# Another order of attention steps, loads and first MLP units in a fused decay-attention and MLP kernel

## The chip, the cores and the metric

The kernel runs on one NeuronCore of a Trainium2 chip. The metric is the time of one execution in device microseconds, as the median of several runs. The engines have the names of the profile: PE (TensorE), DVE (VectorE), ACT (ScalarE), POOL (GpSimd) and SP (SyncE, which issues nearly all DMAs here).

## The reference

Attention with a decaying state, in blocks of 64 positions, for 2 batches of 8 heads with 768 positions of 64 features; then two MLPs over the 1536 tokens of 512 features.

```python
for b in range(nb):
    intra = np.einsum('bhic,bhjc->bhij', qb, kb) * Dmask[None]      # lam ** (i - j), causal
    intra = np.einsum('bhij,bhjd->bhid', intra, vb)
    inter = np.einsum('bhid,bhde->bhie', qb * lam_pow[None], kv_state)
    out[:, :, sl] = intra + inter
    kv_state = lam_block[None, :, None, None] * kv_state + np.einsum('bhsd,bhse->bhde', kb * rev_pow[None], vb)
...
g = x @ w_gate; x = (g * sigmoid(g) * (x @ w_val)) @ w_out          # d_ff 1536
h = x @ w_in;   out = (h * np.cos(h)) @ w_out                       # d_ff 2048
```

Everything is float32. The kernel writes each MLP operand as the sum of a high and a low part in a shorter format and makes each product from three matmuls.

## The kernel before

**Attention.** It works in 12 chunks (numbers 0 to 11, six of each batch) of 128 positions with all heads. A chunk needs three loads of 256 KiB, q, k and v, and six steps on PE, which the code names by a letter and the chunk: `t` transposes q and k in halves of 64 rows (line 1079), `s` makes the scores (1097), `d` the addition to the state (1104), `a` scores times v (1110), `c` q times state (1119; chunks 0 and 6 have none, chunks 5 and 11 no `d`). `m` makes the decay mask once (1088). Between them ACT copies the transposed tiles out of PSUM (tile `qkt`), DVE multiplies the scores with the mask (tile `at`) and updates the state, and POOL makes the decayed copies `kd`, `qd` and `stmp`. The result of a chunk is the MLP input x, split in high and low parts by ACT and DVE.

**MLPs.** The tokens are three blocks of 512 (0, 1, 2). The first units are plain: `gate` and `val`, each for two columns of weights (f = 0, 1) and three blocks, 12 units of 12 matmuls of 512 columns. After them blocks 0 and 1 go together through products of the seven-product kind (Strassen and Winograd's): `q` in the first MLP and `r` in the second, with seven pieces named b, a, c, d, 2, 3, 4, six matmuls of 512 columns each; block 2 does the same with 256 columns, as `h` and `w`. The piece `r.d.12` is piece d of kind r for the weights 12; it adds to the PSUM bank of `r.c.12`, which ACT must have copied out first. Between the pieces stand the down projections, groups of three matmuls. DVE and ACT turn every unit's result into the operand of a down projection, and every loaded weight into its two parts.

**Who sets the order.** The program is written by a scheduler in the kernel that runs at build time: it keeps a clock for each engine, prices each operation and always emits the one that can start first. Each engine then runs its list in order. Three tables steer it. `STEPS` gives the order of attention steps, with `u` where an MLP unit may stand. `LOADS` ranks the loads of q, k, v and the first weights (G0, V0, G1, V1: gate and val for f = 0, 1). `units` lists the units in order. Where the scheduler expects PE to idle for over 1 us before an attention step, it puts in matmuls on zeros (line 234), one for each 115 ns of it. Prices of loads include pauses of 1 us at the times in `FETCHES`.

```python
turn_of = {(names[o[0]], int(o[1:])): n - 1000 for n, o in enumerate(LOADS.split())}
...
BUFS = {"q": 3, "k": 3, "v": 5, "qkt": 2, "qd": 3, "kd": 2, "at": 2, "stmp": 2}
```

Of the kernel before, what the change touches and what calls it, by code (L numbers as in the profile page):

```python
# [47 lines left out]
EARLY = 4  # L48
LATENCY = 130
ISSUE = 400  # L50
STALL, FETCHES = 1000, (13000, 20600, 29000, 36500, 45000, 54500, 63500)
BEHIND = 7000
ATT_NS = {"t": 470, "mask": 700, "s": 892, "st": 464, "av": 875, "qs": 440}
TILES = {"mask": "32", "t": "64*128", "s": "64*128", "st": "128*64", "av": "128*64", "qs": "64*64"}
STEPS = (
# [3 lines left out]
)  # L59
LOADS = (  # L60
    "q0 k0 k1 q1 q3 k2 q4 q2 k3 q5 v0 k4 k6 k5 v1 v2 q6 k7 v3 v4 G0 v5 k8 q7 v6 q8 "
    "v8 v7 k9 q9 q10 k10 k11 q11 V0 v9 v11 v10 V1 G1"
)
HELD = 6, 7, 8, 9
BUFS = {"q": 3, "k": 3, "v": 5, "qkt": 2, "qd": 3, "kd": 2, "at": 2, "stmp": 2}
# [7 lines left out]
def kernel(  # L73
# [222 lines left out]
    ]  # L296
    first2 = len(downs)
    units = [(nm, blk, f) for f in range(GROUP1) for nm in ("gate", "val") for blk in range(NBLK - 1)]
    units += [(nm, NBLK - 1, f) for f in range(GROUP1) for nm in ("gate", "val")]
    parts = "bcad234"  # L300

# [45 lines left out]
    def matrix(kind, f):  # L347

        if kind in "qh":
            return tuple((nm, f) for nm in ("gate", "val", "sa", "sb"))  # L350
        return ("in2", f), ("in2", f + 1), ("ta", f), ("tb", f)

    def work(op):

        if op[0] in ATT_NS:
            return ATT_NS[op[0]] / 1360
        if op[0] in ("h", "w"):
# [55 lines left out]
    for key in list(first_use):  # L413
        if key[0] in ("sa", "sb", "ta", "tb"):
            m = matrix("q" if key[0] in FIRST else "r", key[1])
# [191 lines left out]
    def switch(sub):  # L607

        kind = sub["op"][0]
        if TILES.get(kind) != last_tiles[0]:  # L610
            return SWITCH.get(kind, 145)
        return 60 if last_tiles[1] and kind not in ATT_NS else 0

    def small(sub):

        return sub["op"][0] in ("h", "w")
# [26 lines left out]
    def run_pe(sub, end, idle):  # L643

        unit = any(sub is s for s in pe_units)
        last_small[0] = small(sub)
        last_tiles[:] = TILES.get(sub["op"][0]), sub["op"][0] in ATT_NS
        for subs in (pe_att, pe_units, pe_downs):
            subs[:] = [s for s in subs if s is not sub]
        items = []  # L650
        for _ in range(int(sub["bank"])):
# [3 lines left out]
            if unit:  # L655
                unit_banks.add(item[1])
        sub["fn"](*(items or [None]), **({"idle": idle} if idle and sub["op"][0] in ATT_NS and items else {}))
        for key in sub["keys"]:
# [395 lines left out]
    def att_sub(op):  # L1054
# [92 lines left out]

        return dict(ns=ATT_NS[kind], needs=needs, keys=[], bank=n, fn=fn, then=then, clock=seen[op], op=op)

# [513 lines left out]
```

## Time and profile before

| | |
|---|---|
| time, median of 3 runs (lowest to highest) | 591.8 us (591.25 to 592.13) |
| the profiled execution | 590.59 us |
| its span, first to last instruction | 588.8 us |
| PE busy | 578.5 us, 98% |
| DVE, ACT, POOL busy | 506.0, 362.5, 34.1 us |
| granted TensorE clock, mean | 0.999 |

Busy time is that in which an engine has an instruction at work. The profiled execution is 1.2 us under the median, and 1.8 us of it lie outside the span. The profile's lines are L numbers of the kernel before; the changed kernel's are one higher from line 299 on.

### The profile page before, as it was taken

The numbers are of one execution on the slowest core, as the hardware profiler recorded it, in microseconds if no ns is written. First come the engines' busy times: TensorE is split into PE (matmuls) and PEld (weight loads), VectorE is DVE, ScalarE is ACT, GpSimd is POOL, SyncE is SP. The second block draws the span as 40 slices with busy tenths as digits, with TensorE's granted clock in tenths as the row PEclk, the third lists the DMA queues.
The fourth block names the chain that finished last, engine by engine and source line by source line (L and its number), as shares of the span: only waits on it lengthen the run. The fifth ranks groups of instructions, "written<-read, shape, count | busy, mean of one in ns | idle before, by whom it ended". The sixth has DMA issues, their size and how long they took to land.

```text
span 588.8 us, 9643 instructions
## 1 busy us (share of the span) xinstructions
PE 578.5 (98%) x3620; PEld 491.8 (84%) x3620; DVE 506.0 (86%) x943; ACT 362.5 (62%) x689; POOL 34.1 (6%) x50
## 2 busy tenths in 40 slices
PE   8999999999999999999999999999999999989997
PEld 5888888888888888888888888888888888868886
DVE  4688899878889889786979999969799999999973
ACT  3554767757567557454453679876568667857641
POOL 5646000000000000000000000000000000000000
PEclk9999999999999999999999999999999999999999
DMA  9999362554585554543441522301212031300013
GB/s 189 211 210 212 113 147 71 162 144 147 175 225 185 156 146 140 170 128 141 129 142 51 180 89 72 107 2 39 70 37 71 1 108 37 108 0 1 1 74 141
DMA packets 72816, 66.68 MB, mean 113 GB/s; under 512 B 40002, under 2 KB 60738, under 8 KB 72770
## 3 DMA queue, kind: packets, MB, share of 16 engines
q1 hardware_dynamic: 72768, 66.07, 40.2%
q8 instruction: 28, 0.46, 0.3%
q14 instruction: 18, 0.15, 0.1%
q10 hardware_dynamic: 2, 0.00, 0.0%
HBM read 54.00 MB, written 12.06 MB: 112 GB/s over the span
## 4 chain that ended last, share of the span: by engine, by line
PE 84%; DVE 11%; ACT 2%; DMA 1%; issue 1%; SPq 0%; ACTq 0%; DVEq 0%
PE bank L154 21%; PE bank L155 21%; PE bank L156 20%; PE bank L1493 5%; PE bank L1494 5%; PE bank L1495 5%; DVE s L529 2%; DVE sum L529 2%; PE bank L1110 2%; PE bank L1097 2%; DVE wl L541 1%; DMA v<-in_v_dram 1%; PE bank L1119 1%; PE bank L1079 1%; PE bank L1104 1%; DVE s L1241 1%
## 5 line engine op out<-in xcount | busy, mean ns | idle before, releaser
L154 PE MATMUL bank<-xl,wh 128*128 128x512 f32 (+1 forms) x336 | 118.4, 352 | 3.0 <-ACT s L536 3.0
L536 ACT ACTIVATE s<-s 128x512 f32<-128x512 f32 (+2 forms) x124 | 73.4, 594 | 75.2 <-DVE s L529 47.5
L155 PE MATMUL bank<-xh,wh 128*128 128x512 f32 (+1 forms) x336 | 117.7, 350 | 0.0
L156 PE MATMUL bank<-xh,wl 128*128 128x512 f32 (+1 forms) x336 | 117.3, 349 | 0.0
L536 ACT ACTIVATE s<-bank 128x512 f32<-128x512 f32 (+2 forms) x126 | 62.5, 500 | 36.4 <-PE bank L156 30.8
L536 ACT ACTIVATE gh<-s 128x512 fp32r<-128x512 f32 x84 | 52.7, 628 | 38.7 <-DVE s L529 35.3
L529 DVE TENSOR_TENSOR s<-bank,s 128x256 f32<-128x256 f32 (+1 forms) x102 | 57.3, 563 | 22.2 <-PE bank L156 21.3
L154 PE MATMUL bank<-wl,gh 128*128 128x512 f32 (+1 forms) x196 | 75.6, 386 | 0.0
L155 PE MATMUL bank<-wh,gh 128*128 128x512 f32 (+1 forms) x196 | 75.6, 386 | 0.0
L156 PE MATMUL bank<-wh,gl 128*128 128x512 f32 (+1 forms) x196 | 75.5, 385 | 0.0
L154 PEld LDWEIGHTS bank<-xl,wh 128*128 128x128 f32 x336 | 63.6, 189 | 12.7 <-ACT s L536 3.7
L156 PEld LDWEIGHTS bank<-xh,wl 128*128 128x128 f32 x336 | 63.6, 189 | 8.4
L155 PEld LDWEIGHTS bank<-xh,wh 128*128 128x128 f32 x336 | 63.7, 190 | 8.1
L529 DVE TENSOR_TENSOR sum<-bank,sum 128x512 f32<-128x512 f32 (+1 forms) x97 | 63.2, 681 | 8.1 <-PE bank L156 5.8
L536 ACT ACTIVATE wh<-ct 128x512 fp32r<-128x512 f32 x91 | 55.5, 627 | 23.8 <-DVE ct L205 20.2
L541 DVE TENSOR_TENSOR wl<-ct,wh 128x512 fp32r<-128x512 f32 x91 | 61.3, 688 | 6.9 <-ACT wh L536 6.2
L529 DVE TENSOR_TENSOR gl<-s,gh 128x512 fp32r<-128x512 f32 x84 | 57.7, 689 | 6.3 <-ACT gh L536 5.9
L1493 PE MATMUL bank<-gh,wl 128*128 128x512 f32 x144 | 56.2, 390 | 0.0
L1494 PE MATMUL bank<-gh,wh 128*128 128x512 f32 x144 | 56.2, 390 | 0.0
L1495 PE MATMUL bank<-gl,wh 128*128 128x512 f32 x144 | 56.1, 389 | 0.0
L193 ACT ACTIVATE ct<-raw 128x512 f32<-128x512 f32 x68 | 44.9, 668 | 7.6 <-DMA raw<-in_moe_w_out_dram 4.4
L205 DVE SCALAR_TENSOR_TENSOR ct<-ct,raw 128x512 int32<-128x512 int32 x68 | 46.4, 689 | 3.1 <-ACT ct L193 1.3
(169 smaller groups left out, 1034.7 us busy)
## 6 DMA issues: line engine op xcount, KB each, us to landing
raw<-in_moe_w_out_dram SPq DMA_DIRECT2D x28, 512.0 KB, 3.6
raw<-in_moe_w_in_dram SPq DMA_DIRECT2D x16, 512.0 KB, 3.8
raw<-in_moe_w_gate_dram SPq DMA_DIRECT2D x24, 256.0 KB, 4.6
raw<-in_moe_w_val_dram SPq DMA_DIRECT2D x24, 256.0 KB, 4.5
draftout<-raw SPq DMA_DIRECT2D x9, 512.0 KB, 2.6
q<-in_q_dram SPq DMA_DIRECT2D x12, 256.0 KB, 5.2
k<-in_k_dram SPq DMA_DIRECT2D x12, 256.0 KB, 5.3
v<-in_v_dram SPq DMA_DIRECT2D x12, 256.0 KB, 5.7
```

The lines of the kernel that those rows point to most:

```text
L154: nc.tensor.matmul(ps, wh, xl, start=first, stop=False, **kw)
L155: nc.tensor.matmul(ps, wh, xh, start=False, stop=False, **kw)
L156: nc.tensor.matmul(ps, wl, xh, start=False, stop=last, **kw)
L193: nc.scalar.activation(t, words[:, :, 1].bitcast(F32), AF.Prelu, scale=2.0 ** -112, alpha=2.0 ** 32)
L205: nc.vector.scalar_tensor_tensor(out=w, in0=w, scalar=3, in1=lo, op0=ALU.logical_shift_left, op1=ALU.bitwise_or)
L529: engine, 66 + n * 1.047 if engine == "DVE" else n * 2.45, lambda: unit.tensor_tensor(out=out, in0=in0, in1=in1, op=op),
L536: return go("ACT", (175 if fn == AF.Silu else 40) + n * 0.94, lambda: nc.scalar.activation(out, src, fn, **kw))
L541: return "any", {"DVE": 66 + n * 1.047, "POOL": n * 2.45}, lambda e: (nc.vector if e == "DVE" else nc.gpsimd).tensor_tensor(out=out, in0=i ...
L1097: nc.tensor.matmul(ps[:, p * C:(p + 1) * C], kt[r, p, :], qt[r, p, :], start=True, stop=True)
L1493: nc.tensor.matmul(ps, lo[:, cs], gh, start=first, stop=False)
L1494: nc.tensor.matmul(ps, hi[:, cs], gh, start=False, stop=False)
L1495: nc.tensor.matmul(ps, hi[:, cs], gl, start=False, stop=last)
```

## The change

Three tables and one list change. `FETCHES` and `ATT_NS` are prices in the scheduler's clock and set no wait by themselves. `units[:4]` puts the gate and val units of f = 0 first, for block 0 and then block 1, where before both gate units of f = 0 came first. Six units stand among the attention steps where three stood.

```diff
-STALL, FETCHES = 1000, (13000, 20600, 29000, 36500, 45000, 54500, 63500)
+STALL, FETCHES = 1000, (13471, 21050, 27114, 34715, 41507, 53380, 64222, 69133)
-ATT_NS = {"t": 470, "mask": 700, "s": 892, "st": 464, "av": 875, "qs": 440}
+ATT_NS = {"t": 490, "mask": 700, "s": 892, "st": 464, "av": 875, "qs": 440}
 STEPS = (
-    "t0 m s0 t1 a0 t2 s1 d0 s2 d1 a1 t3 t4 a2 s3 d2 c2 c1 d3 a3 d4 c3 t5 s4 t6 s5 "
...
+    "t0 m s0 t1 s1 t2 d0 s2 t3 a0 a1 d1 s3 c1 t4 d2 a2 c2 d3 a3 t5 s4 c3 s5 d4 a4 "
...
 LOADS = (
...
+units[:4] = [(nm, blk, 0) for blk in range(2) for nm in ("gate", "val")]
```

The instructions of both programs are the same on every engine but for two things: four more matmuls on zeros (44 for 40, with their weight loads), and one `wl` subtraction of 512 columns that goes from DVE to POOL (line 541). All else is order.

**SP, the first loads.** Tile numbers are given by chunk in order of their buffers: q_182, k_183, v_184 are chunk 0, q_185, k_186, v_187 chunk 1, q_188, k_189, v_190 chunk 2. Before:

```order
L936 DMA q_182<-in_q_dram 128x8x64
L936 DMA k_183<-in_k_dram 128x8x64
L936 DMA k_186<-in_k_dram 128x8x64
L936 DMA q_185<-in_q_dram 128x8x64
L936 DMA k_189<-in_k_dram 128x8x64
L936 DMA q_188<-in_q_dram 128x8x64
L936 DMA q_222<-in_q_dram 128x8x64
L936 DMA v_184<-in_v_dram 128x8x64
L936 DMA v_187<-in_v_dram 128x8x64
```

Of the changed kernel, the same place:

```order
L937 DMA q_182<-in_q_dram 128x8x64
L937 DMA k_183<-in_k_dram 128x8x64
L937 DMA q_188<-in_q_dram 128x8x64
L937 DMA k_189<-in_k_dram 128x8x64
L937 DMA k_186<-in_k_dram 128x8x64
L937 DMA q_185<-in_q_dram 128x8x64
L937 DMA q_222<-in_q_dram 128x8x64
L937 DMA v_187<-in_v_dram 128x8x64
L937 DMA v_184<-in_v_dram 128x8x64
L937 DMA v_190<-in_v_dram 128x8x64
L937 DMA k_267<-in_k_dram 128x8x64
```

Chunk 1's q goes from the 4th to the 6th place and chunk 0's v from the 8th to the 9th; chunk 3's k (k_267) is 11th. The last load of attention moves from the 40th place to the 44th, behind G1 and V1.

**PE, the first steps.** Of each step the first matmul of each kind stands. Before:

```order
L1097 MATMUL bank6_247<-qkt_221 128x128
...
L1079 MATMUL bank0_262<-anti_90,q_185 128x64
...
L234 MATMUL bank2_298<-zeros_92 128x256
...
L1110 MATMUL bank2_298<-at_257,v_184 64x128 x4
...
L1079 MATMUL bank4_335<-anti_90,q_188 128x64
...
L1097 MATMUL bank0_359<-qkt_280 128x128
...
L1104 MATMUL bank1_374<-v_184,kd_283 64x64 x8
```

Of the changed kernel; the zero matmuls are 9, 12 and 9 here, and 26 above:

```order
L1098 MATMUL bank6_247<-qkt_221 128x128
...
L234 MATMUL bank0_269<-zeros_92 128x256
...
L1080 MATMUL bank0_269<-anti_90,q_185 128x64
...
L234 MATMUL bank2_305<-zeros_92 128x256
...
L1098 MATMUL bank2_305<-qkt_296 128x128
...
L1080 MATMUL bank4_330<-anti_90,q_188 128x64
...
L1105 MATMUL bank6_353<-v_184,kd_263 64x64 x8
...
L234 MATMUL bank1_385<-zeros_92 128x256
...
L1080 MATMUL bank1_385<-anti_90,q_222 128x64
...
L1111 MATMUL bank4_415<-at_257,v_184 64x128 x4
```

The one stretch of zeros ahead of a0 has become three, ahead of t1, s1 and t3, and a0 stands behind t3.

**PE, the second MLP, from `r.c.12` to `r.d.12`.** Of each piece the first matmul stands. Before (bank 5 is that of c and d):

```order
L154 MATMUL bank5_5827<-t1l_3701,wh_5719 128x512
...
L154 MATMUL bank6_5756<-xl_181,wh_5717 128x256
...
L154 MATMUL bank1_5770<-w2l_4047,wh_5717 128x256
...
L154 MATMUL bank6_5857<-xl_3895,wh_5440 128x512
...
L154 MATMUL bank1_5770<-w3l_4049,wh_5719 128x256
...
L154 MATMUL bank5_5827<-xl_3707,wh_5717 128x512
```

Of the changed kernel (bank 3 is that of c and d):

```order
L154 MATMUL bank3_5760<-t1l_3680,wh_5637 128x512
...
L154 MATMUL bank7_5732<-wl_5160,gh_5563 128x512
...
L154 MATMUL bank6_5803<-w1l_4030,wh_5637 128x256
...
L154 MATMUL bank2_5814<-xl_181,wh_5408 128x256
...
L154 MATMUL bank7_5732<-wl_5452,gh_5641 128x512
...
L154 MATMUL bank2_5814<-w2l_4032,wh_5635 128x256
...
L154 MATMUL bank6_5883<-xl_3905,wh_5408 128x512
...
L154 MATMUL bank3_5760<-xl_3686,wh_5635 128x512
```

Between the first matmul of c and that of d stand 30 matmuls before, five pieces with c itself; now 66, with ten groups of a down projection (`gh`) among them that stood behind d before.

## Rows read from the trace of the kernel before

**Rows 1.** The page: busy times of the engines, and GB/s in 40 slices.

```profile
PE 578.5 (98%) x3620; PEld 491.8 (84%) x3620; DVE 506.0 (86%) x943; ACT 362.5 (62%) x689; POOL 34.1 (6%) x50
...
GB/s 189 211 210 212 113 147 71 162 144 147 175 225 185 156 146 140 170 128 141 129 142 51 180 89 72 107 2 39 70 37 71 1 108 37 108 0 1 1 74 141
```

**Rows 2.** Waits of PE, 0 to 100 and 100 to 589: total us, times, longest.

```profile
PE bank L1110 <- DMA v<-in_v_dram: 1.5, 1, 1.5
PE bank L1097 <- ACT qkt L536: 1.2, 3, 0.6
...
PE bank L154 <- ACT s L536: 3.0, 2, 2.9
```

**Rows 3.** Windows: stretch, length, busy us of PE, PEld, DVE, ACT, POOL; clock, DMA.

```profile
63.77:88.39 24.62, 24.62 (x112) 20.40 (x109) 24.36 (x47) 18.27 (x36) 0.00 (x0) 1.00 0.58 150
...
514.80:517.90 3.10, 0.24 (x3) 0.04 (x1) 3.08 (x7) 2.29 (x5) 0.00 (x0) 1.00 0.00 0
```

**Rows 4.** Timeline of PE in attention: start us, length, work, idle before.

```profile
5.02 0.69 PE L1079 MATMUL bank<-anti,q 64*128 64x64 f32 x8
...
9.16 3.01 PE L234 MATMUL bank<-zeros 128*128 128x256 bf16 x26
13.62 1.09 PE L1110 MATMUL bank<-at,v 128*64 128x128 f32 x16 [1.45 <-DMA v<-in_v_dram]
14.65 0.46 PE L1079 MATMUL bank<-anti,q 64*128 64x64 f32 x8
...
15.19 1.11 PE L1097 MATMUL bank<-qkt 64*128 64x128 f32 x16
16.24 0.69 PE L1104 MATMUL bank<-v,kd 128*64 128x64 f32 x16
...
24.01 1.10 PE L1119 MATMUL bank<-qd,state 64*64 64x128 f32 x32
25.04 0.69 PE L1104 MATMUL bank<-v,kd 128*64 128x64 f32 x16
25.56 1.04 PE L1110 MATMUL bank<-at,v 128*64 128x128 f32 x16
...
49.12 0.50 PE L154 MATMUL bank<-xl,wh 128*128 128x512 f32 x1
...
52.07 0.67 PE L1119 MATMUL bank<-qd,state 64*64 64x128 f32 x16
```

**Rows 5.** Tile views of the 6th load (a q) and the 9th (a v).

```profile
L936 SPq DMA_DIRECT2D q<-in_q_dram x1: 1004/1004/1004, 5.1 to 5.1; - x1
...
DMA to landing us min/median/max: 5.0/5.0/5.0
...
L936 SPq DMA_DIRECT2D v<-in_v_dram x1: 1100/1100/1100, 8.5 to 8.5; - x1
...
DMA to landing us min/median/max: 6.2/6.2/6.2
```

**Rows 6.** Timeline of ACT and DVE from 500 to 520: start, length, work.

```profile
517.27 0.58 ACT L536 ACTIVATE s<-bank 128x512 f32<-128x512 f32 x1
...
502.08 1.29 DVE L541 TENSOR_TENSOR wl<-ct,wh 128x512 fp32r<-128x512 f32 x2
503.28 0.69 DVE L1241 SCALAR_TENSOR_TENSOR s<-s,y 128x512 f32<-128x512 int32 x1
503.89 0.76 DVE L198 TENSOR_SCALAR raw<-raw 128x512 int32<-128x512 int32 x2
504.56 1.29 DVE L205 SCALAR_TENSOR_TENSOR ct<-ct,raw 128x512 int32<-128x512 int32 x2
```

**Rows 7.** Timelines of POOL and DVE around 50 us, working at the same time.

```profile
49.76 1.81 POOL L529 TENSOR_TENSOR qd<-qkt,lrow 128x512 f32<-128x512 f32 x1 [0.59 <-ACT qkt L536]
...
49.74 2.38 DVE L541 TENSOR_TENSOR x<-t,x 128x512 f32<-128x512 f32 x2
52.05 1.28 DVE L541 TENSOR_TENSOR x<-x,x 128x512 f32<-128x512 f32 x2
```

More of the change, by code (lines that the diff above doesn't have):

```diff
@@ L50 @@
 ISSUE = 400
-STALL, FETCHES = 1000, (13000, 20600, 29000, 36500, 45000, 54500, 63500)
+STALL, FETCHES = 1000, (13471, 21050, 27114, 34715, 41507, 53380, 64222, 69133)
 BEHIND = 7000
-ATT_NS = {"t": 470, "mask": 700, "s": 892, "st": 464, "av": 875, "qs": 440}
+ATT_NS = {"t": 490, "mask": 700, "s": 892, "st": 464, "av": 875, "qs": 440}
 TILES = {"mask": "32", "t": "64*128", "s": "64*128", "st": "128*64", "av": "128*64", "qs": "64*64"}
 STEPS = (
[3 rows of a table removed]
[3 rows of a table added]
 )
 LOADS = (
-    "q0 k0 k1 q1 q3 k2 q4 q2 k3 q5 v0 k4 k6 k5 v1 v2 q6 k7 v3 v4 G0 v5 k8 q7 v6 q8 "
-    "v8 v7 k9 q9 q10 k10 k11 q11 V0 v9 v11 v10 V1 G1"
+    "q0 k0 q2 k3 k2 q3 q5 k1 q1 q4 v1 k4 v0 v2 k5 v3 G0 v4 q6 k6 q7 v5 k7 V0 v6 v7 "
+    "k9 v9 q9 k8 q8 G1 k10 q10 V1 k11 q11 v8 v10 v11"
 )
```

4 rows, old and new, of the table STEPS are left out of this document.

## The prediction

> **What bounds the kernel now.** I read the page first. PE is busy for 578.5 of 588.8 us [rows 1], so time can only be won where PE waits or works on zeros. The waits of PE name all of that [rows 2]: in the first 100 us 1.5 us for a load of v and 1.2 us for ACT's copies of transposed tiles, after that one wait of 2.9 us for ACT. The second is in the windows [rows 3]: from 514.80 to 517.90 PE works 0.24 us of 3.10, while DVE works 3.08. The timeline of PE [rows 4] shows the start of attention step by step, the start of one row to the start of the next being the price of a step: 0.54 us for `t`, 1.05 for `s`, 1.03 for `a`, 0.52 for `d`, 0.52 for `c` (1.03 for two), 2.95 for a unit between attention steps. Units in a row cost 2.73 (nine from 63.77 to 88.39, [rows 3]).
>
> With the mask, for which I take 1.1 as for an `s`, 12 t, 12 s, 12 a, 10 d, 10 c and three units make 6.5 + 12.6 + 12.4 + 5.2 + 5.2 + 1.1 + 8.9 = 51.9 us. They begin at 5.02 [rows 4] and end where the nine units begin, at 63.77 [rows 3]: 58.8 us. So 6.9 us are lost there; 4.46 of them stand in one place, from 9.16, where 26 zero matmuls run for 3.01 us and a wait of 1.45 follows, to 13.62 [rows 4]. Late copies take 1.2 more [rows 2]. The GB/s row shows why a new order of loads can only trade: four slices of 14.72 us at 189 to 212 GB/s [rows 1], a queue that never rests while attention loads.
>
> **The change: the start.** The amount of work is the same, so I walk the new order through with the old prices, and with landings by place in the queue, since all these loads have 256 KiB. The 6th load is issued at 5.1 and lands 5.0 later, at 10.1; the 9th at 8.5 and 6.2 later, at 14.7 [rows 5].
> - `t1` now needs the 6th load. Before, s0 ended at about 8.6 (0.6, a `t` with its step to the next, ahead of the zeros at 9.16), and t1 ran at once. Now nine zeros (26 took 3.01, so 0.116 each) end at 9.6, and t1 starts at about 10.15. Lost: 1.6.
> - t1 ends at 10.7; twelve zeros last until 12.1, and ACT's two copies (0.6 each, the price of 512 columns [rows 6]) are done by then. Lost: 1.4.
> - s1, t2, then `d0` with chunk 0's v, the 9th load: at 13.7 it waits until 14.8. Lost: 1.1.
> - d0, s2 until 16.4, nine zeros until 17.45; k of chunk 3, two places behind, has landed by then. Lost: 1.0.
>
> That is 5.1. The rest of the old loss is 6.9 - 4.46 - 1.2 = 1.2, of which I leave 0.7 standing, as belonging to the first transposition and the mask, which do not change; so 5.8. Units stand in five groups, where they stood in four, and each group costs 0.22 once (2.95 - 2.73): 0.2 more. 6.9 - 5.8 - 0.2 = 0.9: the first product begins at 87.5, against 88.4, and attention ends six units earlier, at 71.0. From 17.45 on I find no late load: GB/s [rows 1] puts 44 loads of 0.262 MB (11.5 MB) at about 56 us, and t11, the first that needs one of the last places, comes ten steps before the end of attention, at 61. So the walk says -0.9. It has no late copies in it, of which the old order had 1.2; the steps behind their copies stand farther apart now (t3 and s3 have a0, a1, d1 between them), but V0's first unit follows c7 directly, while DVE makes V0's low part behind two masks and the copies of block 1. I charge 0.4 for that and take -0.5. Bounds: -1.5 if the loads come a little sooner than their places say, +0.8 if all of the 1.2 us of late copies return.
>
> **The place from r.c.12 to r.d.12.** DVE makes the operands here without a break. Before, PE asks for `r.d.12` at 514.8, after 30 matmuls. Its bank must be copied by ACT, at 517.27 for 0.58 us [rows 6], into a buffer `s` that a DVE operation far back in DVE's list frees, and ACT's list has a `gh` in front that waits for the same DVE. I counted in the two programs what lies between a common point (the down projection of weights 9, block 1, which DVE adds up) and that DVE operation: 37 operations of 512 columns and 7 of 256 on DVE, at 0.60 and 0.335 each [rows 6], 24.5 us; on PE 72 matmuls at 0.227 (2.73 / 12) and 48 at 0.12 (an estimate, for half the columns), 22.1 us. DVE is late by 2.4, and the hand-over comes on top of it: that is the 2.9 of [rows 2]. Meanwhile ten groups of a down projection stood ready behind r.d.12, in PE's list. In the new order they stand in front, and the copy's DVE work is done sooner: from the tightest point (`w.3.8`) 78 long and 10 short operations, 50.2 us, against 192 and 78 matmuls, 53.0. PE is 2.8 behind DVE there, where it was 2.4 ahead. The wait of 2.9 goes.
>
> What is late next? The same count over every piece of the new order has its smallest margin at `r.3.12`: 95 long and 15 short, 62.0 us of DVE, against 231 and 84 matmuls, 62.5. PE gets there 0.5 us behind DVE, with a hand-over still to pay, so I charge 0.3 for waits there and elsewhere. Before, the count gave its only other late place at the first `r` pieces, 0.4 us, and there the new order has a margin of 1.0.
>
> **The rest of the edit.** The two price edits cost nothing in themselves; they act through the order. The four zeros are in the walk. `units[:4]` lets a gate meet its val sooner, work for DVE that is moved to a time in which it has none to spare; PE's margin on DVE at the first products stays at 0.5 by the same count, so I put it at nothing; uncovered it would cost one long operation, 0.6. The `wl` on POOL takes 0.60 off DVE at about 73 us, and its price is bounded below by nothing, above by the slowing of two DVE operations [rows 7]: they took 2.38 instead of 1.28 while POOL had one of the same size at work, which itself took 1.81. It belongs to the first product piece, 14 us later, so I take nothing. The Trainium skill, SBUF — State Buffer, section "SBUF: two separate sides", says of DVE operations with two SBUF inputs and a POOL operation that the one that starts first has the shared ports for its whole length and the other is blocked. By that rule DVE would lose up to the whole POOL operation; the two timelines [rows 7] show a loss on both sides instead. Either way the sum stays.
>
> **Sum.** -0.5 - 2.9 + 0.3 = -3.1 against the profiled 590.59, so 587.5; the median is 1.2 above the profiled execution, and 591.8 - 3.1 gives 588.7. DMA issue order on SP shifts behind the start too, but PE waited for no load after 13.62 [rows 2], and the counted room between a load's earliest issue and its use is at least 5.4 us of PE's work (the parts of the weights for r.c.2), no less than the 5.0 that a load took in a queue that was full [rows 5].
>
> **Rivals.** A change of under 0.2%, 1.2 us here, can hardly be told from none.
> - **The wait goes, the start gives nothing** (0.20): late copies of 1.2 come back, +0.8 instead of -0.5. 591.8 + 0.8 - 2.6 = 590.0. For it: ACT's list mixes copies with outputs in both. Against it: the larger distances.
> - **The wait returns in another place** (0.17). DVE works nearly without a break here, and a wait taken from one piece can come up at the next. The margin of 0.5 at r.3.12 is gone if DVE idles 0.5 us in 62. Then -0.5 and about -0.3: 591.0, no difference that can be told.
> - **Slower** (0.09): the same place, with DVE idle for more. The first 3.9 us of idling pay off the margin and what was won (0.5 + 2.9 + 0.5), so it decides from 3.9 of 62 us, 6%. At 9%, 5.6 us, r.3.12 waits 5.1 and the time is 591.8 - 0.5 - 2.9 + 5.1 = 593.5. Against it: from 514.80 to 517.90 DVE idles 0.02 of 3.10 [rows 3], and 14% over the whole run [rows 1] is idleness that comes where PE does not wait for it.
> - **As forecast** (0.54): 588.7, own range 587.0 to 589.7.
>
> **Numbers.** The time of the likeliest is 588.7. The range reaches from 587.0 (the start's -1.5, all of the wait, no new one) to the third case's 591.3. Faster by over 0.2% (under 590.6): the forecast and the first rival but for its edge, 0.73. Within 0.2%: 0.18. Slower: 0.09.
>
> **What would show it.** In the changed kernel's timeline the first transposition of chunk 1 at 10.1 behind nine zeros, d0 at 14.8 after a wait for v, and the first product at 87 to 88. Waits of PE after 100 us: no 2.9 for ACT, and under 0.5 in all. The forecast is wrong if a wait of over 1 us for ACT or DVE stands anywhere from 300 us on, if PE waits for a weight load, or if the steps from 17.45 to 71 stretch by a microsecond or more.

## The result, and the profile after

The changed kernel took 586.82 us (median of 5, 586.15 to 586.94) where the kernel before took 592.13 (median of 5, 591.25 to 592.78): a ratio of 0.9908 with the interval 0.9894 to 0.9923. The prediction was 588.7 with a range of 587.0 to 591.3. The sign was right, and the time is below the range. The profiled execution after took 586.82, so 3.77 less than the 590.59 of the one before.

The page of the changed kernel, to compare with [rows 1], and its waits of PE from 0 to 100 us, to compare with [rows 2]; from 100 us on the view of waits lists none.

```profile
PE 577.8 (99%) x3624; PEld 491.2 (84%) x3624; DVE 502.5 (86%) x942; ACT 364.1 (62%) x689; POOL 35.2 (6%) x51
```

```profile
...
PE bank L1105 <- DMA v<-in_v_dram: 1.0, 1, 1.0
PE bank L1080 <- DMA q<-in_q_dram: 0.7, 1, 0.7
PE bank L1098 <- ACT qkt L537: 0.6, 1, 0.6
...
```

The start, in the timeline of PE after (start, length, work, wait before), to compare with [rows 4]:

```profile
8.26 1.16 PE L234 MATMUL bank<-zeros 128*128 128x256 bf16 x9
10.11 0.47 PE L1080 MATMUL bank<-anti,q 64*128 64x64 f32 x8 [0.69 <-DMA q<-in_q_dram]
...
14.82 0.69 PE L1105 MATMUL bank<-v,kd 128*64 128x64 f32 x16 [0.99 <-DMA v<-in_v_dram]
...
17.61 0.46 PE L1080 MATMUL bank<-anti,q 64*128 64x64 f32 x8
...
29.47 1.16 PE L1098 MATMUL bank<-qkt 64*128 64x128 f32 x16 [0.64 <-ACT qkt L537]
```

And windows, first of the kernel after (from the first product q.b.2 to PE's end, then the stretch that holds the new place of r.d.12), then of the kernel before, from its first product to PE's end (columns as in [rows 3]):

```profile
88.58:581.66 493.08, 493.08 (x2497) 420.93 (x2495) 437.72 (x793) 315.02 (x574) 0.00 (x0) 1.00 0.34 105
...
497.50:514.00 16.50, 16.50 (x85) 14.11 (x84) 16.03 (x29) 13.52 (x26) 0.00 (x0) 1.00 0.30 96
```

```profile
88.39:585.41 497.02, 493.99 (x2497) 421.52 (x2495) 437.12 (x787) 312.58 (x572) 0.00 (x0) 1.00 0.32 102
```

The first product begins 0.19 later than before (88.58, 88.39), so this execution won nothing at the start. From there to PE's end it takes 493.08 instead of 497.02, 3.94 less. Of these 3.03 are time in which PE stood (497.02 - 493.99), nearly all of it the 2.9 us at r.d.12 [rows 2, 3]. The other 0.91 lie inside PE's busy time: the same 2497 matmuls took 493.99 and then 493.08. They are pauses of about 0.1 us, one of them of 0.3, which the view of busy time hides for the most part, since the end of one matmul lies over the next. Told by the starts of the matmuls, eight places of the kernel before have them between 300 and 385 us, and one more is right behind the wait at r.d.12. The largest is at `r.d.0`, which starts 0.56 behind the matmul ahead of it, where 0.23 is usual:

```profile
335.44 0.39 PE L156 MATMUL bank<-xh,wl 128*128 128x512 f32 x1
336.00 0.50 PE L154 MATMUL bank<-xl,wh 128*128 128x512 f32 x1 [0.16 <-ACT s L536]
```

At these first `r` pieces the prediction had counted 0.4 us of lateness before and a margin of 1.0 after, and it left both out of its sum.

In the two profiles, then, the sum is 0.2 - 3.9 = -3.7. The medians differ by 5.3. What makes up the other 1.5 us was the first thing to find out.

### The profile page after: what moved, and what is told of

It is laid out like the page before. It is cut to its first block, busy times and chain, and to the rows that moved or that the text cites. A ratio compares the mean times of both kernels' runs of the same rounds, so it can differ in the third digit from the quotient of the medians.

```text
span 584.9 us, 9692 instructions
## 1 busy us (share of the span) xinstructions
PE 577.8 (99%) x3624; PEld 491.2 (84%) x3624; DVE 502.5 (86%) x942; ACT 364.1 (62%) x689; POOL 35.2 (6%) x51
## 4 chain that ended last, share of the span: by engine, by line
PE 95%; DMA 2%; SPq 1%; issue 1%; DVE 1%; POOL 0%; ACT 0%; DVEq 0%; ACTq 0%
PE bank L154 25%; PE bank L155 24%; PE bank L156 24%; PE bank L1494 6%; PE bank L1495 6%; PE bank L1496 6%; PE bank L1111 1%; PE bank L1098 1%; DMA raw<-in_moe_w_gate_dram 1%; DMA v<-in_v_dram 1%; PE bank L1120 1%; PE bank L1080 1%; SPq L937 1%; PE bank L1105 1%; SPq L172 0%
```

## The experiments

All ran in three groups, each beside the kernel before, whose median was 592.4 to 592.5 in each.

**1. The kernel before against itself.** No edit.

> The kernel before, unchanged, against itself. Open: its profiled execution took 590.59 us and its median 592.13, while the changed kernel's profiled execution is its median. If the waits of the old order differ from execution to execution, this profile shows the wait at r.d.12 with another length than 2.9 us, or waits at other places, and the total of PE's waits after 64 us moves with the span. If the difference lies outside PE's waits, the waits are again 3.0 us after 100 us whatever the time.

592.6 (590.89 to 594.05), ratio 1.0005 (0.9991 to 1.0020). Its profiled execution is 3.4 us longer than that of [rows 1] (span 592.2 for 588.8), with the same order and the same wait of 2.9 at r.d.12. Of the 3.4, 0.7 lie at the start, where PE waits 2.2 for v instead of 1.5 and the first product begins at 89.07 instead of 88.39; the rest lies behind r.d.12. The windows of this execution around that wait, and of [rows 3]'s execution behind its own:

```profile
515.50:518.50 3.00, 0.23 (x2) 0.02 (x1) 2.98 (x6) 2.20 (x5) 0.00 (x0) 0.86 0.00 0
518.50:522.00 3.50, 3.41 (x8) 2.74 (x9) 2.68 (x5) 2.54 (x5) 0.00 (x0) 0.50 0.00 0
522.00:524.50 2.50, 2.50 (x7) 1.92 (x7) 1.08 (x2) 0.72 (x1) 0.00 (x0) 0.50 0.00 0
524.50:526.00 1.50, 1.50 (x9) 1.22 (x8) 1.24 (x3) 0.00 (x0) 0.00 (x0) 1.00 0.00 0
```

```profile
517.90:522.00 4.10, 4.09 (x18) 3.41 (x19) 3.96 (x8) 3.13 (x5) 0.00 (x0) 1.00 0.00 0
522.00:526.00 4.00, 4.00 (x20) 3.30 (x19) 3.36 (x6) 1.78 (x4) 0.00 (x0) 1.00 0.00 0
```

The column before the last two is the granted clock. Toward the end of the wait it falls to 0.50, 1.2 GHz, and stays there up to 524.5: PE does 8 matmuls in 3.50 us, where it did 18 in 4.10 before. The Trainium skill, TensorE: Matmul & The Clock Gate, section "What's actually happening", says that the clock follows how busy PE has been lately and has two levels only. The windows agree, 0.50 and 1.00, with 0.86 where a window holds both.

The mean clock of the executions sorts them. Over this group and the kernel before beside all three groups there are 74: 26 at 0.999 or 1.000 with a median of 591.0, 39 at 0.996 or 0.997 with 592.6, and 9 at 0.993 or 0.994 with 593.7. The profiled execution on which the prediction rests is one of the 26. The one above, at 0.994, is at half clock for 6.8 us. That of experiment 3, at 0.997, is so for about half as long, 3.4 us by this window:

```profile
518.00:522.00 4.00, 3.59 (x10) 2.75 (x10) 3.16 (x6) 1.69 (x3) 0.00 (x0) 0.57 0.00 0
```

**2. The wait of r.d.12 filled with work that isn't used.**

```diff
+        if fill[0]:
+            spare = bank_tile(0)
+            for _ in range(fill[0]):
+                nc.tensor.matmul(spare, wh, xh, start=True, stop=True)
+            fill[0] = 0
         nc.tensor.matmul(ps, wh, xl, start=first, stop=False, **kw)
...
+        fill[0] = 11 if sub["op"] == ("r", "d", 12) else 0
```

> The kernel before with eleven extra matmuls of 512 columns ahead of r.d.12, into a PSUM bank that is free there; their result is not used. They stand in the time in which PE waits (2.86 us, of which they fill 11 x 0.227 = 2.5). Theory A (the granted clock falls behind the wait in about half of the executions, and that is what lifts the median over the best executions): PE never rests for over 0.5 us there, the wait shrinks to about 0.4, every execution shows a clock of 0.999 or 1.000, and the median is that of the old kernel's executions at full clock, 591.0 (ratio about 0.998), with none above 592. Theory B (the spread of the old kernel comes from elsewhere, such as the load of v at the start): the median stays at 592.4, with executions up to 594.

591.24 (590.46 to 593.34), ratio 0.9982 (0.9969 to 0.9994). The timeline of PE in this kernel, at the wait:

```profile
515.01 2.72 PE L159 MATMUL bank<-xh,wh 128*128 128x512 f32 x11
518.04 0.50 PE L161 MATMUL bank<-xl,wh 128*128 128x512 f32 x1 [0.31 <-ACT s L543]
```

r.d.12 begins as late as before (518.04, 517.90), so not a microsecond of work is saved, and the median falls by 1.3. Eight of ten executions are at 0.999 or 1.000, against 4 of 20 of the kernel before beside them. This shows that in most executions the clock falls because PE rests at that place. Two still fell, to 0.997 and 0.996; where, no profile shows.

**3. r.d.12 four groups later.** In the kernel before, with PE's list held as it was but for this:

```diff
-    ... w.3.12 r.d.12 D1.2.11*4 D1.1.10*4 r.2.12 ...
+    ... w.3.12 D1.2.11*4 r.d.12 D1.1.10*4 r.2.12 ...
```

(D1.2.11 is the down projection of the second MLP for block 2 and weights 11, four groups.)

> The kernel before with PE's order of the tail written out, and one piece moved: r.d.12 behind the four groups of the down projection 11 of block 2 that followed it. The step of the prediction (the wait is one of place, the groups behind r.d.12 stood ready): 2.5 to 2.9 us faster than before. Theory A (DVE as a whole is late there): those groups need a DVE subtraction that stands three operations behind r.d.12's in DVE's list, so PE waits for them instead, over 4 us, and the time is that of before or up to 0.6 us more.

592.5, ratio 1.0007 (0.9993 to 1.0021): nothing. The waits of PE from 100 us on:

```profile
PE bank L180 <- ACT gh L562: 2.4, 1, 2.4
PE bank L182 <- DVE gl L555: 0.4, 1, 0.4
PE bank L180 <- ACT s L562: 0.2, 1, 0.2
```

The same 2.8 us are now waited for `gh` and `gl`, the operands of the groups that were put in front. The prediction had said that ten groups "stood ready". These four of the ten did not; the other six were not moved. This fits a DVE that is behind as a whole, and not only for the one buffer of r.d.12.

**4. Half of the change: the old start with the new order, and the new start with the old.** In each, PE's list from the first product on is held to that of the other kernel; the tables of the start stay.

```diff
+TAIL_ORDER = (
+    "q.b.2 q.c.2 q.a.2 q.d.2 h.b.2 h.c.2 h.a.2 q.2.2 D0.0.0*4 q.3.2 D0.0.1*3 q.b.3 q.4.2 h.d.2 h.2.2 D0.0.1 D0.1.0 "
...
+        if not pe_att and not any(s["op"][0] in ("gate", "val") for s in pe_units):
+            sub = next(s for subs in (pe_units, pe_downs) for s in subs if s["op"] == forced[0])
```

The old start with the new order:

> The kernel before up to its twelfth unit, and from the first product on PE's order of the changed kernel, written out; the lists of the other engines follow from the scheduler. If PE's order of the tail alone carries the gain: 586.8 to 587. Theory A: counted in this program, DVE's list differs and is 4.5 us late at q.c.6, near 177 us, and nowhere else by over 0.2, so 4 to 5 us slower than the changed kernel, 591 to 592.

595.24 (595.10 to 595.49), ratio 1.0050 (1.0033 to 1.0066). Its waits from 100 us on, and the windows of the first wait and behind it:

```profile
PE bank L180 <- ACT wh L562: 3.4, 1, 3.4
PE bank L180 <- DVE s L555: 1.0, 2, 0.5
PE bank L182 <- DVE wl L567: 0.2, 1, 0.2
```

```profile
177.00:180.50 3.50, 0.12 (x2) 0.01 (x1) 2.87 (x7) 2.27 (x4) 0.00 (x0) 0.86 0.99 267
180.50:186.00 5.50, 5.31 (x17) 4.21 (x18) 3.93 (x9) 2.50 (x4) 0.00 (x0) 0.50 0.39 145
```

The new start with the old order:

> The changed kernel's attention, loads and first units with PE's list of the old kernel behind the first product. Theory A (DVE's total work against PE's, counted over the whole stretch, sets where PE waits): the wait is no longer at r.d.12 but at the down projection of weights 13, block 0, near 542 us, 2.6 counted and about 3.0 with the hand-over; 1.1 more at q.4.2 near 106 us and 0.6 at r.3.14. That is 586.8 + 4.5 = 591.3, and 1.7 to 3.4 more in the executions in which the clock falls: a median of 591.3 to 593. Theory B (the old order alone makes the wait at r.d.12): the wait stands at r.d.12 with 2.9, no other over 0.5, and the time is that of the kernel before, 592, or 0.5 less by the prediction's start.

592.21 (591.65 to 593.08), ratio 0.9999 (0.9990 to 1.0008). Its waits from 100 us on:

```profile
PE bank L180 <- ACT gh L563: 1.2, 1, 1.2
PE bank L180 <- ACT s L563: 0.9, 1, 0.9
PE bank L180 <- DVE s L556: 0.8, 2, 0.5
```

Neither half is faster than the kernel before; the first is slower. In both, r.d.12 waits for nothing and other places do: near 180 us in the one, at the counted place (the down projection of weights 13, block 0, at 547) and three others in the other, 2.9 us in all by this view. Told by the starts of its matmuls, small pauses included, the second kernel loses 6.0 us behind the first product, where the changed kernel loses 0.3: that is why it takes 592.2 without a fall of the clock. The count named places better than sizes: 2.6 at 547 was 1.2, 1.1 at 106 was 0.5, and 0.6 at r.3.14 did not come. It missed one place, 0.9 us at 382; that PE, having waited there, let DVE catch up before 547 fits, but is not shown. With 1.2 us as its longest wait, all 11 executions of the second kernel are at 0.999 or 1.000; all 6 of the first, with 3.4, are below. PE's order fits the work that DVE has at that time, or it does not, and the start sets which work that is.

**5. More work for DVE in the changed kernel.** One operation is issued six times instead of once, with the same result:

```diff
+AGAIN = 1, 2, 10
...
+            out=y, in0=n_, scalar=-TWO_PI_1, in1=up, op0=ALU.mult, op1=ALU.add) for _ in range(6 if key == AGAIN else 1)], not psum)
```

> The changed kernel with one DVE operation of 512 columns issued five times more than needed (same result), near 490 us: 5 x 0.60 = 3.0 us more work for DVE. Theory A (DVE's work against PE's sets the waits, and the smallest margin there is 0.5): PE waits 2.4 to 3.0 us in all between 490 and 530, at r.3.10, r.2.12 or r.3.12, for DVE or for ACT behind it; 589.2 to 589.8 at full clock, 1.7 more in the executions in which the clock falls. Theory B (the new order gave DVE room, by the 2.8 us counted at r.d.12): no wait over 0.5 and 586.8 to 587.3.

590.78 (589.16 to 591.47), ratio 0.9972 (0.9957 to 0.9986). DVE's timeline where the operation stands, and PE's waits from 100 us on:

```profile
487.24 4.32 DVE L1241 SCALAR_TENSOR_TENSOR y<-s 128x512 f32<-128x512 int32 x6
```

```profile
PE bank L155 <- DVE s L531: 2.6, 1, 2.6
```

3.0 us of work made a wait of 2.6 at r.3.10, 495 us: of all the work of DVE there only 0.4 us lay beside spare time. The executions fall in two: 4 of 12 at 0.999 or 1.000, 589.2 to 589.5, so 2.6 over the changed kernel; 8 at 0.996 or 0.997, 590.7 to 591.5. This is the kernel before in small: the wait, and behind it 1.9 more (medians 589.4 and 591.3) in most executions.

**6. Without the line `units[:4]`**, all else changed:

```diff
-    units[:4] = [(nm, blk, 0) for blk in range(2) for nm in ("gate", "val")]
```

> The changed kernel without the one line units[:4]; STEPS, LOADS and prices stay, so the start of attention is the new one up to the first units. Theory A (the time is set by the waits of PE for DVE in the tail): counted in this program, DVE is 3.0 us late at the unit in2.2.2, near 360 us, and nowhere else by over 0.8, so about 3.4 us slower than the changed kernel, 590.0. Theory B (the new start and loads bring the gain): as the changed kernel, 586.8.

595.02 (594.13 to 597.08), ratio 1.0054 (1.0035 to 1.0072). Its waits, from 0 and from 100 us on, and two windows:

```profile
PE bank L154 <- DVE xl L529: 2.3, 1, 2.3
...
PE bank L154 <- DVE s L529: 2.9, 2, 1.9
```

```profile
46.00:49.50 3.50, 3.49 (x9) 2.78 (x10) 3.35 (x9) 0.47 (x2) 0.94 (x1) 0.54 1.16 190
...
362.00:368.00 6.00, 3.13 (x13) 1.95 (x11) 6.00 (x11) 4.83 (x10) 0.00 (x0) 1.00 0.01 3
```

The second unit stands right behind c7. Without the line it is a gate for block 1, whose x DVE has not finished: 2.3 us of waiting and 3.5 at half clock, so that the first product begins at 92.6 instead of 88.6. With the line it is the val of block 0, which needs nothing new, and at 44.12 it started without a wait. Of the further 2.9 at 362 to 368 the count had said 3.0. A line that the prediction put at nothing carries 8 us in this order of steps; it has to be said that without it the scheduler orders everything behind it anew, and that part of the 8 is this.

**7. The changed kernel with the old prices** (`FETCHES`, and 470 for `t`):

```diff
-STALL, FETCHES = 1000, (13471, 21050, 27114, 34715, 41507, 53380, 64222, 69133)
-ATT_NS = {"t": 490, "mask": 700, "s": 892, "st": 464, "av": 875, "qs": 440}
+STALL, FETCHES = 1000, (13000, 20600, 29000, 36500, 45000, 54500, 63500)
+ATT_NS = {"t": 470, "mask": 700, "s": 892, "st": 464, "av": 875, "qs": 440}
```

> The changed kernel with the old prices (FETCHES and the price of t), all tables new. Theory A (the prices matter only through order, and this order has no place where the count finds DVE late): no wait of PE over 0.5 us after 100 us and 586.8, within 0.6. Theory B (the new prices are needed to keep PE ahead): a wait of 1 us or more for DVE or ACT after 100 us, and 588 to 593.

586.61 (586.34 to 587.33), no wait from 100 us on: no difference to the changed kernel's 586.8 can be told, so the prices are worth nothing that shows, as predicted.

**8. The start.** The changed kernel and three others, these with PE's list from the first product on held to that of the changed kernel. The changed kernel once more:

> The changed kernel itself, for its spread beside the others of this group. Theory A (no wait behind the start that lets the granted clock fall): every execution at a clock of 0.999 or 1.000, 586.2 to 587.2. Theory B (its first five executions were lucky): some executions 1.7 or 3.4 us longer at 0.997 or 0.994, as the kernel before has them.

586.8 (586.08 to 588.16), six of six at 1.000. In its profiled execution the first product begins at 87.84, 0.74 sooner than in the profile after. The rows of ACT that decide it, first of the profile after, then of this execution (the last row of the second group is PE's, s5):

```profile
27.60 0.68 ACT L193 ACTIVATE ct<-raw 128x512 f32<-128x512 f32 x1 [0.95 <-DMA raw<-in_moe_w_gate_dram]
28.17 0.27 ACT L537 ACTIVATE x<-bank 128x128 f32<-128x128 f32 x1
28.33 1.08 ACT L537 ACTIVATE qkt<-bank 128x512 f32<-128x512 f32 x2
```

```profile
26.59 0.72 ACT L193 ACTIVATE ct<-raw 128x512 f32<-128x512 f32 x1
...
27.34 1.10 ACT L537 ACTIVATE qkt<-bank 128x512 f32<-128x512 f32 x2
...
28.69 1.16 PE L1098 MATMUL bank<-qkt 64*128 64x128 f32 x16
```

ACT works its list in order. `ct<-raw` needs the gate weights; where they land late, ACT stands for 0.95 us, with the copies of t5 behind it, and s5 begins at 29.47 instead of 28.69. The landing of a weight that no attention step needs costs the attention 0.8 us.

d4 ahead of s5:

```diff
-    "... d3 a3 t5 s4 c3 s5 d4 a4 "
+    "... d3 a3 t5 s4 c3 d4 s5 a4 "
```

> The changed kernel with d4 ahead of s5 in the attention's steps, and PE's list behind the first product held as it is. Theory A (the start lost its forecast gain to late copies: s5 waits 0.64 for ACT's copies of t5): d4 fills 0.5 of that wait, the first product begins at 88.1 instead of 88.58 and the median falls from 586.8 to 586.3. Theory B (the copies are late whatever stands ahead, or the loads hold the start): the wait moves to a4, t6 or a later step, the first product stays at 88.5 and the time at 586.8.

586.49 (586.17 to 587.20, 4 executions). s5 waits no more, and from t3 to the first unit it takes 14.5 us instead of 15.1, but no difference to the changed kernel's 586.8 can be told. In the profiled execution the first product begins at 88.96, later than any expected, because s0 and the zeros behind it ran slowly in it and t3 began 0.97 late (last section). With the old prices as well:

> The changed kernel with d4 ahead of s5 and the old prices, PE's list behind the first product held as it is. Theory A (s5's wait is the one thing that the start loses behind t3): from t3 to the first unit it takes 14.1 to 14.5 us instead of 15.1, and the median is 586.3, 0.3 to 0.6 under the changed kernel of the same group. Theory B (loads later in the queue give it back): 586.8 like the changed kernel.

589.21 (588.43 to 589.69). Here the scheduler moved other steps, twelve zeros and a wait of 1.4 at s7 among them, and the first product begins at 91.0: it tells nothing of the question.

Last, the loads in the order of the chunks and no zeros ahead of t1, s1 and t3:

```diff
-    "t0 m s0 t1 s1 t2 d0 s2 t3 a0 a1 d1 s3 c1 t4 d2 a2 c2 d3 a3 t5 s4 c3 s5 d4 a4 "
+    "t0 m s0 t1 a0 s1 t2 d0 a1 s2 d1 c1 t3 a2 s3 d2 c2 t4 a3 d3 c3 s4 t5 d4 a4 s5 "
...
-    "q0 k0 q2 k3 k2 q3 q5 k1 q1 q4 v1 k4 v0 v2 k5 v3 G0 v4 q6 k6 q7 v5 k7 V0 v6 v7 "
+    "q0 k0 q1 k1 v0 q2 k2 v1 q3 k3 v2 q4 k4 v3 G0 q5 k5 v4 q6 k6 q7 v5 k7 V0 v6 v7 "
```

> The changed kernel with another start and PE's list behind the first product held: loads in the order q0 k0 q1 k1 v0 q2 k2 v1 q3 k3 v2, and t1 right behind s0, a0 behind that, where 9, 12 and 9 zeros stood. Theory A (the walk by places in the queue is right, and 5.1 us are lost in the first 18 us to loads that come late by their place): t3 is done with a0, a1, d1 and c1 behind it by 17.6, the first product begins at 86 to 87 and the time is 584.5 to 585.5. Theory B (the queue of loads as a whole sets the pace of the start, whatever order): what is won ahead of t3 is lost at s3 to s5, the first product begins at 88 to 89 and the time is 586.3 to 587.3.

586.70 (586.12 to 587.53), the first product at 88.40: the numbers of the second theory. The walk's part of it came true, with t3 at 17.59 behind a0, a1, d1 and c1, 3 us of work more than in the changed kernel by then (fifteen zeros stand ahead of a0). All of it is given back. The waits of PE from 6 to 100 us, and ACT's list ahead of s3 and around the longer wait, at s4:

```profile
PE bank L1136 <- ACT qkt L560: 2.3, 2, 1.4
PE bank L1118 <- DMA k<-in_k_dram: 0.6, 1, 0.6
```

```profile
18.89 0.78 ACT L560 ACTIVATE x<-bank 128x128 f32<-128x128 f32 x4
...
24.84 0.70 ACT L216 ACTIVATE ct<-raw 128x512 f32<-128x512 f32 x1 [0.92 <-DMA raw<-in_moe_w_gate_dram]
25.43 0.77 ACT L560 ACTIVATE x<-bank 128x128 f32<-128x128 f32 x4
26.06 0.63 ACT L560 ACTIVATE qkt<-bank 128x512 f32<-128x512 f32 x1
```

Again the gate weights hold ACT, and the copy for s4 waits behind them; then t7 waits for its k. The 0.9 at s3 is of another kind: there ACT makes four copies of x between the two of `qkt`, and no load is waited for. So about half of what was given back goes to loads, 0.9 and 0.6 us, and the rest to the order of ACT's list; the second theory, which names the loads alone, is right in its number only. Three quite different starts (88.39 before, 88.58 and 87.84 after, 88.40 here) reach the first product within 0.8 us of each other.

## Why the prediction was wrong

**The step that failed is the last one of the sum**: "the median is 1.2 above the profiled execution, and 591.8 - 3.1 gives 588.7". It carries the distance between median and profiled execution over to a kernel that lacks its cause. Experiments 1 and 2 show the cause: the clock falls to 1.2 GHz in about two executions of three (48 of 74), behind the wait at r.d.12 in the one that was profiled, and in 2 of 10 with that wait filled; the profile ahead of the prediction showed one in which it had not fallen, as its clock of 0.999 said. So the wait was priced at 2.9 where in the median it cost 2.9 and 1.4 more (592.4 against 591.0). Once it is gone the median lies at or little above the profiled executions, 586.8 beside 586.82 and 586.08. The profile alone gave 590.59 - 3.1 = 587.5, which is 0.7 from the result, but partly by luck: of its terms the start was 0.7 too good for that execution and the small waits 1.2 too bad.

Two terms were mis-sized, the clock by 1.4 and the new small waits by 1.2. The time lies only 0.2 below the range, so with either of them right it would have lain inside. The lower end of the range is not what its own terms give, either: 591.8 - 1.5 - 2.9 is 587.4, not 587.0; and the third case is priced at 591.0 among the rivals and at 591.3 in the range.

**The wait at r.d.12 goes, -2.9**: right, and the reason held, DVE's work counted against PE's. Experiment 5 put 3.0 us of work into the counted margin and got 2.6 of waiting. One sentence of it was wrong, that PE had ready groups behind r.d.12 (experiment 3); moving r.d.12 behind the first four of them was worth nothing.

**New small waits, +0.3**: there were none, and 0.9 us of small pauses went too, mostly of the kind that the view of waits does not list. So this term should have been -0.9; its sign was wrong, though the count had named the first `r` pieces, where part of it lay. The margin of 0.5 at r.3.12 held, so the rival in which the wait returns elsewhere fell with it, and the slower one; experiments 4 and 6 show that both were real: with one part of the change missing the wait did return, and the time was 592.2, 595.0 or 595.2.

**The start, -0.5**: in place to 0.2 us (t1 at 10.11 for 10.15, d0 at 14.82 for 14.8, t3 at 17.61 for 17.45), then up to 0.8 lost at s5 that the walk did not have, since it left ACT's list out. The profiles give +0.19 and, of the second execution, -0.55. With the old start the first product began at 88.4 to 89.1 in five profiles and with the new one at 87.8 to 88.6 in four (the second kernel of experiment 4 and experiment 5 among them), so about -0.3 in the mean; the term is right within what executions differ by. The rival in which the start gives nothing had the wrong total for the same reason as the forecast.

**`units[:4]` at nothing**: wrong as a price of the line (experiment 6), without harm to the sum, since the walk had the line's order in it.

**The `wl` on POOL, nothing**: right in the sum; it takes 1.48 us at 72.6, and PE waits for nothing behind it. The prediction's reading of [rows 7] was wrong. It says that the two timelines show a loss on both sides "instead" of the rule that it cites from the Trainium skill, by which one operation has the shared ports and the other is blocked. Taken one by one, the two DVE operations, and POOL's operation of the same kind when undisturbed, are these:

```profile
49.74 0.68 DVE L541 TENSOR_TENSOR x<-t,x 128x512 f32<-128x512 f32 x1
50.34 1.78 DVE L541 TENSOR_TENSOR x<-t,x 128x512 f32<-128x512 f32 x1
```

```profile
46.30 1.27 POOL L529 TENSOR_TENSOR qd<-qkt,lrow 128x512 f32<-128x512 f32 x1 [0.23 <-ACT qkt L536]
```

The first DVE operation ran as usual. POOL's, issued at 49.76, took 1.81, its own 1.27 and 0.54 to about the end of the first. The second DVE operation, from 50.34, ended at 52.12, 0.55 behind POOL's end at 51.57. Each was held once by the other, and the rows agree with that rule.

In medians, then: start -0.3, wait -2.9, small pauses -0.9, clock -1.4, together -5.5 of 592.4 - 586.8 = 5.6.

How often the clock fell, beside the longest wait of PE from 38 us on in the profiled execution:

| kernel | longest wait, us | executions below 0.999 |
|---|---|---|
| changed | none | 0 of 11 |
| d4 ahead of s5; old prices | none | 0 of 4 each |
| d4 ahead of s5, with the old prices | 1.4, at s7 | 0 of 6 |
| the last start of experiment 8 | none | 1 of 5 |
| before, with the wait filled | 0.3 | 2 of 10 |
| new start, old order | 1.2 | 0 of 11 |
| without the units line | 2.3 | 6 of 8 |
| r.d.12 later | 2.4 | 10 of 12 |
| more work for DVE | 2.6 | 8 of 12 |
| before | 2.9 | 48 of 74 |
| old start, new order | 3.4 | 6 of 6 |

What stays open: why the same wait lets the clock fall in one execution and not in the next, where the clock fell in the two executions of experiment 2 and in one of five of the last start, and why one execution of experiment 6 took 596.7 us at full clock.

## What to carry to other kernels

A wait of PE of two to three microseconds can cost up to twice its length: look in several executions, not in one, whether the granted clock falls behind it, and if the median lies above a profiled execution at full clock, take that distance for a part of the wait's price. When two engines are as close as PE and DVE here (0.4 us of spare time over many microseconds of work), an order belongs to its start: judge both together, by the summed work between a common point and each place where one engine needs the other. And where loads hold up a start, look through each engine's list in order for an instruction that waits for a load which the step behind it does not need.

## What the runs showed of the hardware

The granted clock of a window does not tell all at the very start. In the profiled execution with the old prices s0 took 2.08 us, in the profile after 1.16; its matmuls ran at about half speed, while the windows from 5 us on show 1.00 in both:

```profile
7.40 2.08 PE L1098 MATMUL bank<-qkt 64*128 64x128 f32 x16
```

```profile
7.17 1.16 PE L1098 MATMUL bank<-qkt 64*128 64x128 f32 x16
```

The 1.00 is no measurement there: the first record of the clock in the trace begins at 11.2 us in the one execution and at 5.7 in the other, and the view counts the time ahead of it as full clock. So at the start go by the length of the matmuls.

What this costs depends on what stands behind. With the old prices t3 began at 17.92, against 17.61 in the profile after, since there are no zeros ahead of t3 in that kernel. In the kernel with d4 ahead of s5, which has nine there, the start was as slow, and t3 began 0.97 late:

```profile
7.40 2.08 PE L1139 MATMUL bank<-qkt 64*128 64x128 f32 x16
...
18.58 0.47 PE L1121 MATMUL bank<-anti,q 64*128 64x64 f32 x8
```
